# The product with w_out1 in groups of three tiles (384 columns), one block of output rows at a time

## Chip, core and metric

The kernel runs on one core of a Trainium2 chip. The metric is the device time of one launch in microseconds (us). It is written in Bass and Tile; the engines are TensorE (PE), VectorE (DVE), ScalarE (ACT), GpSimd (POOL) and SyncE (SP), which issues most DMAs. Each engine takes its instructions strictly in the order in which the program emits them.

## What is computed

The reference, cut to what matters:

```python
x = attention(q, k, v)                  # chunks of 64 rows, 8 x 8 heads, 4608 rows of 512 in all
h = x @ w_in                            # 512 -> 1024
e = np.exp(h - h.max(-1)); solu = h * e / e.sum(-1)
ln = (solu - mean) / np.sqrt(var + 1e-06) * g_ln
y = ln @ w_out                          # 1024 -> 512: "the product with w_out1"
h2 = y @ w_in2                          # 512 -> 2048
return (np.maximum(h2, 0) + alpha * np.minimum(h2, 0)) @ w_out2
```

## The kernel before

The 4608 rows are 36 tiles of 128. Phase 1 takes each tile through attention, the projection with `w_in`, SoLU, layer norm and the product with `w_out1`; the result `y` (transposed, 512 rows in four row blocks of 128) goes to DRAM. Phases 2 and 3 are the second feed-forward part and are not touched. Every fp32 product of this kind is three matmuls of rounded halves (`mm3`: high x high, high x low, low x high).

The order of all work in phase 1 is written by hand as tables of names with a tile number. `FIRST` lists the start (tiles 0 to 9), `STEP` is one step of the loop over tiles i = 10 to 35, in which `name+d` works on tile (or y step) i+d, and `LAST` is the end. The names that matter here: `q`, `qk`, `qm`, `qe`, `tr`, `te`, `pv`, `xn`, `xt` are attention; `xh` (ACT) and `xl` (DVE) split its result into high and low halves; `hm` is the projection (24 matmuls of 512 columns, line 483; below "projection t" for tile t); `hx` (DVE maximum), `he` (ACT exponential), `so` (DVE), `sq` (ACT square), `zv`, `pw` (POOL), `zs` (DVE) are SoLU and layer norm; `zt` transposes the result on PE into PSUM, `zh` (ACT) and `zl` (DVE) write its halves; `ya`, `yb` are the two halves of a y step, and `ye` (ACT) copies its result from PSUM and issues the store to DRAM. `conv` in `STEP` converts one unit of the second part's float64 weights (`p` on ACT, `l` on DVE, `s`, `a` on POOL) and, with `run_post`, splits earlier units (`hi` on ACT, `lo` on POOL). Steps 20, 24 and 28 (`twice`) convert a second unit, whose ACT work (`hi` of earlier units, then `p`) stands between `sq` and `xh`.

A projection can start only when `so` of the tile before has read its PSUM banks (`ps_h` has one buffer) and when its own `xh` is there; the loads and copies around it run ahead.

y groups: two tiles (`YT` = 2) share one pair of buffers `zh`, `zl` of 256 columns, three pairs in all. Each tile index s is a y step of two of the four row blocks of its group, `ya` the one and `yb` the other: 24 matmuls of 256 columns each. Both write one PSUM bank (`ps_y`, one buffer), and `ye` copies it in one ACT instruction of 512 columns. A second bank (`ps_y2`) is there for `LAST` alone. At the very start the float64 pieces of `w_in` and the halves of tiles 2 to 5 (`wraw`, `xe`) lie in the y buffers, which are not yet used.

Of the kernel before, what the change touches and what calls it, by code (L numbers as in the profile page):

```python
# [42 lines left out]
def order(text):  # L43
# [18 lines left out]
    f19 qs10 s16 zt3 h15 o15 l16 v11 hx4 s18 he4 p17 so4 A16 sq4 f21 s17 ya0 yb0 zv4 hm5 p20 ye0 zh3  # L62
    l17 ya1 yb1 pw4 l18 hm6 hx5 f22 he5 p19 qn10 a17 ye1 zs4 zl3 so5 a18 p21 xh8 sq5 S19 zv5 zt4 pw5
    h18 zs5 ya2 yb2 zh4 hx6 he6 h17 o18 zt5 zl4 l19 zh5 so6 o17 sq6 zv6 pw6 zl5 hm7 s20 zs6 zt6 ye2
    h16 hx7 he7 so7 xh9 xl8 zh6 sq7 ya3 yb3 zv7 S21 l20 pw7 zs7 hm8 tr10 zl6 hx8 zt7 qk11 a19 te10
    pv10 xl9 he8 f23 so8 sq8 zh7 hm9 qm11 zv8 ye3 zl7 xh10 hx9 ya4 yb4 pw8 qe11 zs8 he9 so9 sq9 h19
# [23 lines left out]
def tile_chunk_attention_solu_prelu(  # L90
# [75 lines left out]
    def phase1():  # L166
        with ExitStack() as c1, ExitStack() as c0:
# [416 lines left out]
            def yevac(s):
                assert ("yb", s) in done
                j, half = divmod(s, 2)
                y = yp.tile([128, 2, YG], F32, name="ysb", tag="ysb")
                nc.scalar.activation(out=y, in_=ypend.pop(s), func=AF.Copy)  # L588
# [520 lines left out]
```

## Time and profile before

| what | value |
|---|---|
| median of 3 runs (lowest to highest) | 1315.21 us (1315.11 to 1317.88) |
| the profiled execution: time, span | 1316.45 us, 1314.6 us |
| granted TensorE clock, mean over the span | 0.991 |
| busy PE, PEld, DVE, ACT, POOL | 96%, 89%, 72%, 52%, 25% of the span |
| phase 1 | 0 to 596.5 us |

The span runs from the first instruction to the last; the profiled execution's own time is 1.85 us longer. PE is busy nearly throughout, so what moves the end is PE work taken away or put in, and each wait that PE gains or loses. PEld are weight loads, which overlap the matmuls.

### The profile page before, as it was taken

The page shows a single profiled execution, that of the slowest core. Times are in us where ns is not written, and L with a number is a line of the kernel's source. Part 1 is how long each engine was busy: PE and PEld are TensorE (multiplying, and loading weights), DVE is VectorE, ACT ScalarE, POOL GpSimd, SP SyncE. Part 2 cuts the span into 40 slices and gives each one's busy share as a digit, 9 for nine tenths or more (in the row PEclk, how much of TensorE's full clock was granted, in tenths as well). Part 3 has the DMA queues.
Part 4 walks back from the last instruction along what each step waited for, and adds up shares of the span by engine and source line. Part 5 has one row for each costly group of instructions (what it writes and reads, how often), then busy time and mean ns, then how long its engine had stood idle before and what let it go on. Part 6 is the DMA issues. An engine that isn't in the chain of part 4 may idle for free. (4 is left out here: it accounts for less than half of the span.)

```text
span 1314.6 us, 21447 instructions
## 1 busy us (share of the span) xinstructions
PE 1264.9 (96%) x7968; PEld 1165.5 (89%) x7968; DVE 951.4 (72%) x1425; ACT 689.4 (52%) x1140; POOL 328.1 (25%) x311
## 2 busy tenths in 40 slices
PE   5889899999999999999999999999989999999998
PEld 4778789999889989899999999999989888888898
DVE  6996677776877666535777777777765968768684
ACT  4685355555555555434666666666534344434443
POOL 4574245343656464322020202110000000000000
PEclk9799999999999999999999999999998999999999
DMA  9774167675767573279442433427994738375462
GB/s 235 165 178 112 60 172 183 161 172 153 206 190 212 156 209 107 87 273 351 168 161 98 163 116 143 156 105 273 324 332 158 266 100 275 123 244 188 137 232 96
DMA packets 215496, 237.87 MB, mean 181 GB/s; under 512 B 89312, under 2 KB 174816, under 8 KB 213344
## 3 DMA queue, kind: packets, MB, share of 16 engines
q1 hardware_dynamic: 205440, 226.28, 55.5%
q10 hardware_dynamic: 9792, 9.44, 2.1%
q8 instruction: 63, 1.03, 0.3%
q0 software_dynamic: 160, 0.79, 0.1%
q14 instruction: 41, 0.34, 0.1%
HBM read 149.68 MB, written 86.77 MB: 180 GB/s over the span
## 5 line engine op out<-in xcount | busy, mean ns | idle before, releaser
L804 DVE SCALAR_TENSOR_TENSOR g<-ng,nal,g 128x384 f32<-128x384 f32 x192 | 126.2, 657 | 62.5 <-ACT g L682 62.4
L162 PE MATMUL yps<-zh,wo_h 128*128 128x256 f32 x576 | 167.4, 291 | 0.7 <-ACT ysb L588 0.7
L164 PE MATMUL yps<-zh,wo_l 128*128 128x256 f32 x576 | 162.9, 283 | 0.0
L163 PE MATMUL yps<-zl,wo_h 128*128 128x256 f32 x576 | 162.8, 283 | 0.0
L682 ACT ACTIVATE ng<-g 128x384 f32<-128x384 f32 x144 | 75.8, 526 | 131.7 <-DVE g L676 131.7
L765 PE MATMUL hz<-th,w 128*128 128x384 f32 x384 | 113.5, 336 | 4.4 <-DVE wv L676 4.2
L765 PE MATMUL hv<-th,w 128*128 128x384 f32 x384 | 113.5, 336 | 2.5 <-DVE g L676 2.3
L765 PE MATMUL hx<-th,w 128*128 128x384 f32 x384 | 112.9, 334 | 0.0
L162 PEld LDWEIGHTS yps<-zh,wo_h 128*128 128x128 f32 x576 | 110.3, 192 | 1.0 <-ACT ysb L588 0.9
L163 PEld LDWEIGHTS yps<-zl,wo_h 128*128 128x128 f32 x576 | 110.4, 192 | 0.1
L164 PEld LDWEIGHTS yps<-zh,wo_l 128*128 128x128 f32 x576 | 110.2, 191 | 0.0
L963 PE MATMUL oz<-rhi,w 128*128 128x512 f32 (+1 forms) x304 | 94.7, 372 | 0.6 <-DVE osb L676 0.6
L963 PE MATMUL ox<-rhi,w 128*128 128x512 f32 (+1 forms) x304 | 94.9, 373 | 0.0
L963 PE MATMUL ov<-rhi,w 128*128 128x512 f32 (+1 forms) x304 | 93.7, 369 | 0.0
L682 ACT ACTIVATE rhi<-rt 128x1024 fp32r<-128x1024 f32 (+1 forms) x56 | 54.6, 984 | 63.1 <-DVE rt L679 19.7
L679 POOL TENSOR_TENSOR yt<-y,y 128x384 f32<-128x384 f32 x24 | 26.9, 1143 | 238.8 <-DMA y<-yd 138.9
L682 ACT ACTIVATE g<-g 128x384 f32<-128x384 f32 x144 | 75.2, 522 | 3.1
L563 DVE TENSOR_TENSOR zl<-zt,zh 128x1024 fp32r<-128x1024 f32 x36 | 44.0, 1221 | 45.2 <-ACT zh L558 45.2
L765 PEld LDWEIGHTS hz<-th,w 128*128 128x128 f32 x384 | 70.7, 188 | 6.4 <-ACT th L682 4.7
L765 PEld LDWEIGHTS hv<-th,w 128*128 128x128 f32 x384 | 70.7, 188 | 4.6 <-DVE g L676 2.9
L483 PE MATMUL h<-wi_h,xh 128*128 128x512 f32 x256 | 70.9, 399 | 3.6 <-DVE sl L511 3.4
L679 DVE TENSOR_TENSOR rlo<-rt,rhi 128x1024 fp32r<-128x1024 f32 (+1 forms) x56 | 62.4, 1124 | 15.0 <-ACT rhi L682 14.7
(187 smaller groups left out, 3357.8 us busy)
## 6 DMA issues: line engine op xcount, KB each, us to landing
gd<-g SPq DMA_DIRECT2D x192, 192.0 KB, 1.9
w<-wid SPq DMA_DIRECT2D x8, 1792.0 KB, 9.4
w<-wod SPq DMA_DIRECT2D x8, 1792.0 KB, 9.9
rc<-gd SPq DMA_DIRECT2D x24, 512.0 KB, 3.9
rd<-gd SPq DMA_DIRECT2D x24, 512.0 KB, 4.8
raw<-in_moe_w_out SPq DMA_DIRECT2D x24, 511.8 KB, 4.3
qt<-in_q SPq DMA_DIRECT2D x36, 256.0 KB, 5.1
kbd<-in_k SPq DMA_DIRECT2D x72, 128.0 KB, 5.0
```

The costliest lines, as they stand in the source:

```text
L162: nc.tensor.matmul(o, lh, rh, start=first, stop=False)
L163: nc.tensor.matmul(o, lh, rl, start=False, stop=False)
L164: nc.tensor.matmul(o, ll, rh, start=False, stop=last)
L483: nc.tensor.matmul(ps[:, n], xh[:, kk], w[:, kk, 512 * n:512 * n + 512], start=(kk == 0 and w is wi_h), stop=False,)
L563: nc.vector.tensor_tensor(out=zl, in0=ps, in1=zh.bitcast(F32), op=ALU.subtract)
L679: eng.tensor_tensor(out=out, in0=a, in1=b, op=ALU.subtract)
L682: nc.scalar.activation(out=out, in_=in_, func=func, **k)
L765: nc.tensor.matmul(self.ps[x], w[:, a, i, k], d[:, k], start=(p not in CHAINED and k + j == 0), stop=(k == 1 and j == 2), skip_group_check ...
L804: nc.vector.scalar_tensor_tensor(out=self.g[t], in0=self.n[t], scalar=nal_sb[:, f:f + 1], in1=self.g[t], op0=ALU.mult, op1=ALU.add)
L963: nc.tensor.matmul(bank[key, m][:, :n], W[2 * j + k][:, a, i, 128 * m:128 * m + 128], d[:, k], start=(p not in CHAINED and j + k + q == 0) ...
```

## The change

A y group becomes three tiles (384 columns, `YT` = 3), with two pairs of buffers instead of three. The unit of work is one row block of a group: 24 matmuls of 384 columns. A group has three tile indices and four blocks: each index does one block, `ya` its first 12 matmuls and `yb` the other 12, and the first index of a group does one more block, `yc`, copied by `yd`. Each block is copied and stored by itself (384 columns). In the loop `yc` stands on PE between `qk` and `pv`, `yd` on ACT between `qe` and `so`. 1728 matmuls of 256 columns become 1152 of 384 columns; 36 copies and stores become 48. Of the tables `FIRST` and `LAST` a few entries are shown; how they move the instructions stands below.

```diff
-YT = 2
+YT = 3
 YG = 128 * YT
-YL = 6
...
-    f19 qs10 s16 zt3 h15 o15 l16 v11 hx4 s18 he4 p17 so4 A16 sq4 f21 s17 ya0 yb0 zv4 hm5 p20 ye0 zh3
+    f19 qs10 s16 zt3 h15 o15 l16 v11 hx4 s18 he4 p17 so4 A16 sq4 f21 s17 yc0 zv4 hm5 p20 yd0 zh3
...
-    zv9 qs11 qn11 A20 pw9 xl10 zs9 zt8 o16
+    zv9 qs11 qn11 A20 pw9 xl10 zs9 ye3 zt8 ya4 yb4 o16
...
 STEP = order(
     """
-    q+3 v+3 ye-6 zh-2 zl-2 conv+0 hm+0 tr+1 te+1 qk+2 hx+0 he+0 qm+2 qe+2 pv+1 zt-1 xn+1 so+0 sq+0
+    q+3 v+3 ye-6 zh-2 zl-2 conv+0 hm+0 tr+1 te+1 qk+2 yc-5 hx+0 he+0 qm+2 qe+2 yd-5 pv+1 zt-1 xn+1 so+0 sq+0
     ya-5 conv+1 xt+1 xh+1 xl+1 zv+0 pw+0 qs+2 zs+0 yb-5
     """
 )
...
-            ztp = R("zt", YL // 2)
+            ztp = R("zt", 2)
...
-            rawt = [
-                ztp.tile([128, 2, 512, 4], U16, name=f"wraw{kk}", tag="zh" if kk % 2 == 0 else "zl")
-                for kk in range(K1)
-            ]
-            xt = [ztp.tile([128, 2, 2, NP, 128], F32R, name=f"xe{k}", tag=t) for k, t in enumerate(("zh", "zl"))]
+            rawt = [ztp.tile([128, 3, 512, 4], U16, name=f"wraw{k}", tag=t) for k, t in enumerate(("zh", "zl"))]
+            rx = ztp.tile([128, 3, 2, NP, 128], F32R, name="rx", tag="zh")
+            xe = ztp.tile([128, 3, 2, NP, 128], F32R, name="xe", tag="zl")
...
-            def ymm(s, m):
+            def block(s, extra):
+                j, r = divmod(s, YT)
+                return j, 0 if extra else 1 + r
+
+            def ymm(s, extra, k0, k1):
+                j, m = block(s, extra)
...
-                if m == 0:
-                    ypend[s] = ypools[(s + 1) % len(ypools)].tile([128, 2, YG], F32, name="yps", tag="yps")
+                if k0 == 0:
+                    ypend[j, m] = ypools[m % len(ypools)].tile([128, 512], F32, name="yps", tag="yps")[:, :YG]
...
-                for kk in range(KF1):
-                    mm3(ps, wo_h[:, kk, c], wo_l[:, kk, c], zh[:, kk], zl[:, kk], kk == 0, kk == KF1 - 1)
+                c = slice(m * 128, (m + 1) * 128)
+                for kk in range(k0, k1):
+                    mm3(
+                        ypend[j, m], wo_h[:, kk, c], wo_l[:, kk, c], zh[:, kk], zl[:, kk], kk == 0, kk == KF1 - 1
+                    )
...
+                yc=lambda s: s % YT or ymm(s, True, 0, KF1), yd=lambda s: s % YT or yevac(s, True),
```

Two places show how the order moves (the changed kernel's line numbers are shifted by a few). On ACT, from the exponential of tile 7 (line 503, then 506) to the square of tile 9 and the weight splits behind it; `ysb` is a copy of y, `eh,st<-h` an exponential, `eh,st<-sl` a square. Before:

```order
L503 ACTIVATE eh,st<-h,st 128x1024
L469 ACTIVATE xh<-xd 128x512
L558 ACTIVATE zh<-zt 128x8x128
L519 ACTIVATE eh,st<-sl,st 128x1024
...
L519 ACTIVATE eh,st<-sl,st 128x1024
L238 ACTIVATE hi<-f_1432 128x512
L238 ACTIVATE hi<-f_1103 128x512
L238 ACTIVATE hi<-s_1361 128x512
L588 ACTIVATE ysb<-yps 128x512
```

Now:

```order
L506 ACTIVATE eh,st<-h,st 128x1024
L597 ACTIVATE ysb<-yps 128x384
L599 DMA yd_65<-ysb 128x384
L472 ACTIVATE xh<-xd 128x512
L561 ACTIVATE zh<-zt 128x8x128
L522 ACTIVATE eh,st<-sl,st 128x1024
...
L522 ACTIVATE eh,st<-sl,st 128x1024
L237 ACTIVATE hi<-f_1358 128x512
L237 ACTIVATE hi<-f_1101 128x512
L597 ACTIVATE ysb<-yps 128x384
L599 DMA yd_65<-ysb 128x384
L237 ACTIVATE hi<-s_1313 128x512
```

A copy of y (`ye2`) stands ahead of the work behind the exponential of tile 7, and another (`ye3`) behind two splits.

On PE, from the end of projection 9 to projection 10 (each pair of lines 162 and 164, now 161 and 163, stands for a run of y matmuls: before one of 48, now two of 24 around `zt`). Before:

```order
L489 MATMUL h<-wi_h,xl 128x512 x8
L162 MATMUL yps<-zh,wo_h 128x256
...
L164 MATMUL yps<-zh,wo_l 128x256
L545 MATMUL zt<-ident,sl 128x128 x8
L483 MATMUL h<-wi_h,xh 128x512 x4
```

Now:

```order
L492 MATMUL h<-wi_h,xl 128x512 x8
L161 MATMUL yps<-zh,wo_h 128x384
...
L163 MATMUL yps<-zh,wo_l 128x384
L548 MATMUL zt<-ident,sl 128x128 x8
L161 MATMUL yps<-zh,wo_h 128x384
...
L163 MATMUL yps<-zh,wo_l 128x384
L486 MATMUL h<-wi_h,xh 128x512 x4
```

Here two blocks stand where one step stood. Ahead of it, one block follows each of projections 4, 5 and 6 instead of one step each, and two blocks follow projection 7 instead of one step.

## Rows read from the trace of the kernel before

**Rows 1.** Busy time by engine in a stretch of the loop, then clock, DMA share, GB/s

```profile
200.00:300.00 100.00, 100.00 (x788) 91.13 (x787) 71.00 (x120) 54.18 (x85) 43.28 (x38) 1.00 0.70 167
```

**Rows 2.** Timeline of PE, step 17: start, length, line, tiles, count

```profile
280.53 1.09 PE L483 MATMUL h<-wi_h,xh 128*128 128x512 f32 x4
...
287.46 1.04 PE L439 MATMUL xr<-vbd,ets 128*64 128x128 f32 x16
...
289.28 0.36 PE L162 MATMUL yps<-zh,wo_h 128*128 128x256 f32 x1
289.48 0.28 PE L163 MATMUL yps<-zl,wo_h 128*128 128x256 f32 x1
...
292.24 0.60 PE L459 MATMUL x<-ident,e 128*128 128x128 f32 x4
...
295.55 1.09 PE L483 MATMUL h<-wi_h,xh 128*128 128x512 f32 x4
```

**Rows 3.** Timeline of PE in phase 2, matmuls of 384 columns

```profile
651.00 0.33 PE L765 MATMUL hv<-th,w 128*128 128x384 f32 x1
...
652.04 0.33 PE L765 MATMUL hx<-th,w 128*128 128x384 f32 x1
```

**Rows 4.** Timeline of PE at the start: projections 6 to 11

```profile
121.95 1.09 PE L483 MATMUL h<-wi_h,xh 128*128 128x512 f32 x4
...
138.73 1.19 PE L483 MATMUL h<-wi_h,xh 128*128 128x512 f32 x4 [3.44 <-DVE sl L511]
...
152.57 1.09 PE L483 MATMUL h<-wi_h,xh 128*128 128x512 f32 x4
...
162.55 1.19 PE L483 MATMUL h<-wi_h,xh 128*128 128x512 f32 x4
...
174.69 0.48 PE L483 MATMUL h<-wi_h,xh 128*128 128x512 f32 x1
...
190.43 0.86 PE L483 MATMUL h<-wi_h,xh 128*128 128x512 f32 x3
```

**Rows 5.** Timeline of DVE: `so` of tile 5, attention's scaling in step 17

```profile
119.77 1.28 DVE L511 SCALAR_TENSOR_TENSOR sl<-h,st,eh 128x1024 f32<-128x1024 f32 x1
...
289.01 0.68 DVE L450 TENSOR_TENSOR e<-xr,r 128x512 f32<-128x512 f32 x1
```

**Rows 6.** Timeline of PE in LAST: the second y step, the first matmul of phase 2

```profile
566.73 0.38 PE L162 MATMUL yps<-zh,wo_h 128*128 128x256 f32 x1 [0.69 <-ACT ysb L588]
...
596.49 0.34 PE L765 MATMUL hx<-th,w 128*128 128x384 f32 x1
```

**Rows 7.** Timeline of ACT behind projection 9

```profile
172.86 1.15 ACT L519 ACTIVATE eh<-sl,st 128x1024 f32<-128x1024 f32 x1 [2.00 <-DVE st L514]
...
174.01 1.13 ACT L238 ACTIVATE hi<-f 128x512 fp32r<-128x512 f32 x2
```

**Rows 8.** Timeline of ACT in step 17: the square, then the split of x

```profile
291.56 1.15 ACT L519 ACTIVATE eh<-sl,st 128x1024 f32<-128x1024 f32 x1 [1.80 <-DVE st L514]
...
292.88 0.60 ACT L469 ACTIVATE xh<-x 128x512 fp32r<-128x512 f32 x1
```

**Rows 9.** Timeline of ACT, steps 21 and 24

```profile
354.54 0.58 ACT L469 ACTIVATE xh<-x 128x512 fp32r<-128x512 f32 x1
...
397.52 1.15 ACT L519 ACTIVATE eh<-sl,st 128x1024 f32<-128x1024 f32 x1 [1.80 <-DVE st L514]
...
401.01 0.59 ACT L469 ACTIVATE xh<-x 128x512 fp32r<-128x512 f32 x1
```

**Rows 10.** Timeline of PE: projections 21, 29 and 30

```profile
340.75 1.20 PE L483 MATMUL h<-wi_h,xh 128*128 128x512 f32 x4
...
461.82 1.14 PE L483 MATMUL h<-wi_h,xh 128*128 128x512 f32 x4
...
478.71 0.50 PE L483 MATMUL h<-wi_h,xh 128*128 128x512 f32 x1
```

**Rows 11.** Busy time by engine and clock in a stretch, as Rows 1

```profile
139.00:144.00 5.00, 5.00 (x16) 3.92 (x16) 2.46 (x3) 1.69 (x3) 1.68 (x2) 0.66 0.32 115
```

More of the change, by code (lines that the diff above doesn't have):

```diff
@@ L61 @@
     pv9 h14 hm4 qm10 a13 h13 f18 f17 v12 o12 O13 p16 o14 sq3 l15 zv3 qe10 A15 pw3 zs3 f20 p18 v10
-    f19 qs10 s16 zt3 h15 o15 l16 v11 hx4 s18 he4 p17 so4 A16 sq4 f21 s17 ya0 yb0 zv4 hm5 p20 ye0 zh3
[L63 to L66, printed above, removed]
-    zv9 qs11 qn11 A20 pw9 xl10 zs9 zt8 o16
+    f19 qs10 s16 zt3 h15 o15 l16 v11 hx4 s18 he4 p17 so4 A16 sq4 f21 s17 yc0 zv4 hm5 p20 yd0 zh3
+    l17 ya0 yb0 pw4 l18 hm6 hx5 f22 he5 p19 qn10 a17 ye0 zs4 zl3 so5 a18 p21 xh8 sq5 S19 zv5 zt4 pw5
+    h18 zs5 ya1 yb1 zh4 hx6 he6 h17 o18 zt5 zl4 l19 zh5 so6 o17 sq6 zv6 pw6 zl5 hm7 s20 zs6 zt6 ye1
+    ya2 yb2 h16 hx7 he7 so7 ye2 xh9 xl8 zh6 sq7 yc3 zv7 S21 l20 pw7 zs7 hm8 tr10 zl6 hx8 zt7 qk11 a19 te10
+    pv10 xl9 he8 f23 so8 sq8 zh7 hm9 qm11 zv8 yd3 zl7 xh10 hx9 ya3 yb3 pw8 qe11 zs8 he9 so9 sq9 h19
+    zv9 qs11 qn11 A20 pw9 xl10 zs9 ye3 zt8 ya4 yb4 o16
     """
@@ L567, in phase1, with yevac @@
             ypools = [ps_y]
-            def ymm(s, m):
-                j, half = divmod(s, 2)
-                assert ("zl", 2 * j + 1) in done and all(("o", u) in done for u in range(UI, UO))
+            def block(s, extra):
[3 more added lines that the diff above has]
+                j, m = block(s, extra)
+                assert ("zl", YT * (j + 1) - 1) in done and all(("o", u) in done for u in range(UI, UO))
                 zh, zl = ztt[j]
-                if m == 0:
-                    ypend[s] = ypools[(s + 1) % len(ypools)].tile([128, 2, YG], F32, name="yps", tag="yps")
+                if k0 == 0:
+                    ypend[j, m] = ypools[m % len(ypools)].tile([128, 512], F32, name="yps", tag="yps")[:, :YG]
                 else:
                     assert ("ya", s) in done
-                ps = ypend[s][:, m]
-                c = slice((2 * half + m) * 128, (2 * half + m + 1) * 128)
-                for kk in range(KF1):
-                    mm3(ps, wo_h[:, kk, c], wo_l[:, kk, c], zh[:, kk], zl[:, kk], kk == 0, kk == KF1 - 1)
-                if half and m:
-                    del ztt[j]
[L584 to L588, printed above, removed]
+                c = slice(m * 128, (m + 1) * 128)
[3 more added lines that the diff above has]
+                    )
+                if m == K1 - 1 and k1 == KF1:
+                    del ztt[j]
+            def yevac(s, extra):
+                j, m = block(s, extra)
+                assert ("yc" if extra else "yb", s) in done
+                y = yp.tile([128, YG], F32, name="ysb", tag="ysb")
+                nc.scalar.activation(out=y, in_=ypend.pop((j, m)), func=AF.Copy)
                 g, o = divmod(j * YG, 2 * SG)
-                nc.scalar.dma_start(out=y_dram[g][:, 2 * half:2 * half + 2, o:o + YG], in_=y)
+                nc.scalar.dma_start(out=y_dram[g][:, m, o:o + YG], in_=y)
             for t in (kbd[0], vbd[0]):
```

19 lines of the change are left out of this document (12 added, 7 removed).

## The prediction

> **What bounds the kernel now.** First the busy time by stretches: in the loop of phase 1 PE is busy for all of 100 us at full clock while VectorE has 71, ScalarE 54 and GpSimd 43 of it [rows 1]. So PE's own work sets the time there, as long as the work of the other engines that PE needs back stays shorter than PE's work in between. The timeline of PE in one step shows how the 15.02 us from projection 17 to projection 18 (280.53 to 295.55) are spent, and where its two y pieces lie [rows 2]. The timelines of ScalarE and VectorE show how close they run behind it [rows 5, 8]. The start is another matter: before projection 7 PE stands still for 3.44 us, waiting for VectorE (`so`, line 511) [rows 4]. There PE work is free, and taking it away is worth nothing.
>
> **The price of a y matmul.** In rows 2 the y matmuls start 0.12 us apart: from 289.48 to the transposes at 292.24 there are 23 starts in 2.76 us. A piece of 24 takes 289.28 to 292.24, 2.96 us: 24 x 0.12, and 0.08 for its first one behind transposes. Phase 2 has 384 columns against other weights: six starts from 651.00 to 652.04, 0.1733 us each [rows 3]. So 256 columns cost 0.120 and 384 cost 0.1733: 0.0533 for each 128 and 0.0133 fixed. The product costs 1728 x 0.120 = 207.4 us before and 1152 x 0.1733 = 199.7 after: 7.7 us less PE work. [...]
>
> A block is now 24 x 0.1733 = 4.16 us, in the loop 4.24 in one piece or 2 x 2.16 in two. The 12 additional pieces (`yc`) add 0.08 each, 1 us in all at most; those in the loop are in the lengths below.
>
> **Steps of the loop.** Without y a step has 15.02 - 2 x 2.96 = 9.10 us of PE work. Two steps of three now take 9.10 + 2 x 2.16 = 13.42 (1.60 less), the third 13.42 + 4.24 = 17.66 (2.64 more). Steps 11 to 34 hold 16 short ones and 8 long ones: -25.6 + 21.1 = -4.5 us, if PE never waits. Does it wait? The next projection needs `xh`, on ScalarE behind `sq`. In step 17 `sq` starts 11.03 us after the projection (291.56) and `xh` ends at 293.48, 12.95 after it; PE came 2.07 us later [rows 8]. That chain hangs on the projection (maximum, exponential, `so`, `sq`), not on y, so a short step leaves 13.42 - 12.95 = 0.5 us: no wait. In a long step `pv` comes 4.24 us later (6.93 + 4.24 = 11.17 after the projection), lasts about 1.0, and VectorE's scaling of it (`xn`) stands ahead of `so`; before, `xn` started at 289.01 and `sq` 2.55 us behind [rows 5]. `sq` then starts at about 11.17 + 1.0 + 0.2 + 2.55 = 14.9, `xh` ends near 16.8, under 17.66: no wait. The additional copy `yd` stands on ScalarE between `qe` and `sq` and waits for `yc`; `sq` has to wait longer anyway, which hides it. Without that cover it would cost its half microsecond eight times over.
>
> The double steps 20, 24 and 28 are different. There two splits and a second unit's conversion stand between `sq` and `xh`: in step 24 `sq` starts at 397.52 and `xh` ends at 401.60, 4.08 us later [rows 9]. With `sq` at 11.03, `xh` ends at 15.11: PE's 15.02 just about covered that. A short step 24 reaches the next projection after 13.42 and waits 1.7. Step 28 is short too; I take it at 1.5, its splits being a little shorter. Step 20 is long: 14.9 + 4.08 = 18.98 against 17.66, a wait of 1.3. Before, the three had waits of 0.4 together. Step 21 follows one: `xh` ended at 355.12, 14.37 after projection 21 (340.75) [rows 9, 10], because VectorE was late from step 20; short, it waits 0.9. Step 29 took 16.89 before (461.82 to 478.71) [rows 10], 1.9 more than the rule, for the same lateness; it is a long step now and absorbs it. Net: 1.7 + 1.5 + 1.3 + 0.9 - 0.4 - 1.9 = +3.1 us. The loop: -4.5 + 3.1 = -1.4.
>
> **The start.** Before, three y steps stood ahead of projection 7; now three blocks, 4.16 instead of 5.76 us each. What PE saves there it waits, since `so` of tiles 4, 5 and 6 decide. Only projection 6 comes earlier: it started at 121.95 behind y, and `so` of tile 5 ended at 121.05 [rows 4, 5], so up to 0.8 us is won, and I carry it through to projection 7 at 137.9 (the chain in between starts at projection 6). The work left out there is put in later:
> - Projection 7 to 8 took 13.84 us with one step (5.84). Two blocks now, 2 x 4.16 + 0.08, and between them the copy `ye2`, since there is one PSUM bank. The same handover in `LAST` left PE idle for 0.69 us [rows 6]; I take 0.75. 13.84 - 5.84 + 8.40 + 0.75 = 17.2: projection 8 at 155.1.
> - Projection 8 to 9 held no y: 9.98, as before. Projection 9 at 165.1.
> - Projection 9 to 10: `ya3 yb3`, `zt8`, `ya4 yb4`. The second block waits for `ye3`, which stands on ScalarE behind `sq` of tile 9 and two splits. `sq` started 172.86 - 162.55 = 10.31 us behind projection 9, the splits end at 175.14, 12.59 behind it [rows 4, 7]; with 0.6 for the copy the block starts 13.2 after projection 9, about 2.5 us after PE is ready for it. With 4.2 for the block projection 10 comes after 17.4, at 182.5; before it came at 174.69.
> - Projection 10 to 11 took 15.74 because VectorE came late; with projection 10 so much later it won't be, and the step is short: 13.42. Projection 11 at 195.9 instead of 190.43: +5.5 us.
>
> The other edits of the start cost nothing: the pieces of `w_in` in other buffers have the same loads in the same order; `zh` of tile 3 must now wait for projection 5 (its buffer holds the halves of tile 5), but ScalarE waits for VectorE there anyway. DMAs: 12 more stores of y on ScalarE's queue, none on SP's.
>
> **The end.** From projection 35 on there were six y steps (34.6 us), now eight blocks (33.3): -1.3. Phase 2 began without a wait at 596.49 [rows 6], and its operands are prepared from rows of y stored long before, so this is kept. The one wait at the handover of the bank (0.69) stays.
>
> **Sum.** +5.5 - 1.4 - 1.3 = +2.8 us, and 0.3 for a little less luck with the clock (below): +3.1. The profiled execution took 1316.45, 1.24 over the median of the runs; I put the sum on both alike: 1319.6 for an execution like it, **1318.3 us** for the median.
>
> **Bounds of what no row shows.** How far y of 384 columns differs from phase 2's: from 0.1733 to 1.5 x 0.120 = 0.180, 0 to +7.7 us; I take the former, a row of the same engine and width. The handovers behind `ye2` and `ye3`: from 0.69 each [rows 6] to the 3.44 of the longest wait here [rows 4]; I take 0.75 and 2.5. Together these move the sum from 1.9 less to 3.6 more.
>
> **Rivals.**
> (A) *Faster: the postponed blocks cost nothing.* If the blocks behind projections 7 and 9 fell into waits that PE has there anyway, the start would keep its own saving (8 blocks for 6 steps: -1.3), and the kernel ends at -1.3 - 1.4 - 1.3 = -4.0, 1311.2 us. For it: PE did wait in the start. Against it: the wait of 3.44 lies ahead of the postponed blocks, and behind it projection 8 followed y without an idle time in its row. It decides if projection 11 starts before about 190. 0.10.
> (B) *No change: the double steps don't wait.* If ScalarE reaches `xh` of steps 20, 24, 28 in time, the loop comes to -4.5 - 1.9 - 0.4 + 0.9 = -5.9 instead of -1.4: 1313.8. For it: ScalarE is half idle. Against it: in step 24 it goes from `sq` to `xh` without an idle time in its rows. 0.22.
> (C) *Slower still: the clock.* PE idles for about 5.5 us around the transposes ahead of projection 7 and 2.5 ahead of `ya4`. Before, after the 3.44 us wait, the clock granted from 139 to 144 was 0.66 of full [rows 11], part of the time at 1.2 instead of 2.4 GHz: 5 x 0.34 = 1.7 us. Once or twice more makes 1320.0 to 1321.7. 0.18. The Trainium skill (TensorE: Matmul & The Clock Gate, "Part 1: The HAM clock gate") says that the throttled state is the default and activity releases it; the row agrees.
> (D) *The width is no saving.* With the matmul's time in proportion to its columns, 0.180, nothing is saved on PE: +7.7, 1326.0. Rows 3 speak against it. 0.03. [...]
>
> **Chances.** My forecast has 0.45, by itself from 1316.3 to 1320.3; others 0.02. A measurement of this kernel tells about 0.2% (2.6 us) from no change. The forecast lies near that bound (1317.8): of its 0.45 I give 0.27 to slower, 0.18 to the same. With C and D slower has 0.48; with B and the rest the same has 0.41; A makes 0.11 faster. Range 1313.5 to 1321.2: it holds the forecast, B and most of C.
>
> **What will show it.** Rows of y matmuls 0.173 apart. Projections 11 and on: intervals of 13.4, 13.4, 17.7. Projection 11 near 196, with an idle PE ahead of the second blocks behind projections 7 and 9, put down to the copy `ysb`. Steps 20, 24 and 28 at about 19.0, 15.2 and 15.0. Phase 2 starts near 599.5. I am wrong if projection 11 starts before 193, if the double steps keep the rule, or if phase 2, which isn't touched, takes another time.

## The result, and the profile after

The changed kernel takes 1335.27 us (median of four runs, 1330.28 to 1336.05) where the kernel before took 1315.8 in the same session: a ratio of 1.0139, 95% interval 1.0115 to 1.0163. It is slower by some 19 us; the forecast was 1318.3, at most 1321.2. The profiled execution has a span of 1334.2 us and took 1336.0.

The matmul count fell as the change says, and PE's busy time did not. The sums on the page of the kernel before (busy us, share of the span, count):

```profile
PE 1264.9 (96%) x7968; PEld 1165.5 (89%) x7968; DVE 951.4 (72%) x1425; ACT 689.4 (52%) x1140; POOL 328.1 (25%) x311
```

The page of the changed kernel, first its sums, then the three groups of y matmuls (busy, mean ns of one, idle time before them; matmuls overlap, so the mean is longer than the 174 ns from one start to the next):

```profile
PE 1266.0 (95%) x7392; PEld 1157.9 (87%) x7392; DVE 950.2 (71%) x1425; ACT 689.2 (52%) x1152; POOL 327.1 (25%) x311
...
L161 PE MATMUL yps<-zh,wo_h 128*128 128x384 f32 x384 | 134.5, 350 | 3.6 <-ACT ysb L597 3.6
L163 PE MATMUL yps<-zh,wo_l 128*128 128x384 f32 x384 | 128.8, 335 | 0.0
L162 PE MATMUL yps<-zl,wo_h 128*128 128x384 f32 x384 | 128.8, 335 | 0.0
```

The timeline of PE shows where the time went. These rows answer to [rows 4] and [rows 6] (L486 is the projection, L776 phase 2, L974 phase 3); they are the first matmuls of projections 4, 7, 8, 9, 10, 11 and 35, of phase 2 and of phase 3. The second fence has the three of the kernel before that no group ahead shows: projections 4 and 35 and phase 3.

```profile
99.54 0.48 PE L486 MATMUL h<-wi_h,xe 128*128 128x512 f32 x1
...
141.67 2.08 PE L486 MATMUL h<-wi_h,xh 128*128 128x512 f32 x4 [3.19 <-DVE sl L514]
...
160.18 1.08 PE L486 MATMUL h<-wi_h,xh 128*128 128x512 f32 x4
...
170.18 0.50 PE L486 MATMUL h<-wi_h,xh 128*128 128x512 f32 x1
...
187.51 0.39 PE L486 MATMUL h<-wi_h,xh 128*128 128x512 f32 x1
...
201.46 0.39 PE L486 MATMUL h<-wi_h,xh 128*128 128x512 f32 x1
...
566.90 1.08 PE L486 MATMUL h<-wi_h,xh 128*128 128x512 f32 x4
...
608.33 0.33 PE L776 MATMUL hx<-th,w 128*128 128x384 f32 x1
...
977.79 0.33 PE L974 MATMUL ox<-fhi,w 128*128 128x384 f32 x1
```

```profile
96.03 0.48 PE L483 MATMUL h<-wi_h,xe 128*128 128x512 f32 x1
...
553.78 0.40 PE L483 MATMUL h<-wi_h,xh 128*128 128x512 f32 x1
...
956.56 0.33 PE L963 MATMUL ox<-fhi,w 128*128 128x384 f32 x1
```

| stretch | before, us | after, us | difference | forecast |
|---|---|---|---|---|
| start to projection 4 | 96.03 | 99.54 | +3.5 | 0 |
| projections 4 to 11 | 94.40 | 101.92 | +7.5 | +5.5 |
| projections 11 to 35 (the loop) | 363.35 | 365.44 | +2.1 | -1.4 |
| projection 35 to phase 2 | 42.71 | 41.43 | -1.3 | -1.3 |
| phase 2 | 360.07 | 369.46 | +9.4 | 0 |
| phase 3 to the end of the span | 358.04 | 356.41 | -1.6 | 0 |

The largest term is phase 2, in which no line of code is changed. Two of its units have waits that the kernel before does not have (timeline of PE, then of DVE):

```profile
629.99 0.45 PE L776 MATMUL hx<-th,w 128*128 128x384 f32 x1 [2.77 <-ACT s L693]
...
641.07 0.45 PE L776 MATMUL hx<-th,w 128*128 128x384 f32 x1 [2.37 <-ACT s L693]
```

```profile
627.45 0.56 DVE L687 TENSOR_TENSOR g<-hz,u 128x384 f32<-128x384 f32 x1 [5.15 <-DMA gd<-g]
...
632.60 0.56 DVE L687 TENSOR_TENSOR g<-hv,wv 128x384 f32<-128x384 f32 x1 [1.08 <-DMA gd<-g]
...
637.80 0.56 DVE L687 TENSOR_TENSOR g<-hz,u 128x384 f32<-128x384 f32 x1 [2.38 <-DMA gd<-g]
```

PE waits for ScalarE, which waits for VectorE, and VectorE waits until stores of `g` (`gd<-g`) free one of the six buffers of `g`. Of the units of 42 matmuls the third and the fourth take 11.5 and 12.0 us where the kernel before has 7.3 and 7.7. Why are the stores late? The queue of SP, first of the kernel after, then of the kernel before: `w<-wid` are loads of the weights of phase 2, 1792 KB each. A row of several DMAs runs from the first issue to the end of the last.

```profile
608.40 1.27 SPq L712 DMA_DIRECT2D w<-wid  x3
...
615.11 1.32 SPq L820 DMA_DIRECT2D gd<-g  x2
616.48 5.80 SPq L738 DMA_DIRECT2D y<-yd  x4
622.38 4.86 SPq L820 DMA_DIRECT2D gd<-g  x2
```

```profile
585.09 11.91 SPq L701 DMA_DIRECT2D w<-wid  x3
603.28 1.31 SPq L809 DMA_DIRECT2D gd<-g  x2
604.64 2.00 SPq L727 DMA_DIRECT2D y<-yd  x4
```

Before, the first two of these three loads are issued 11.4 and 11.0 us ahead of phase 2 (596.49) and the third at its start; now all three are issued at its start (608.33), and the first stores of `g` follow 6.7 us later, when the first load has not landed yet. The view of DMA issues of these two stretches (KB each, median us to landing) shows what that costs the stores: 12.0 us after the change, 1.9 before.

```profile
gd<-g SPq DMA_DIRECT2D x2, 192.0 KB, 12.0
```

```profile
gd<-g SPq DMA_DIRECT2D x3, 192.0 KB, 1.9
```

In these stretches every DMA of SP's queue lands behind the one issued ahead of it: after the change the third load lands at 626.85 and the two stores at 627.36 and 627.87; before, the third load lands 0.55 us after the first store is issued. The Trainium skill (DMA: Bandwidth & Descriptors, "Queues, rings and completion order") says that a DMA engine consumes the descriptors of one issuing queue in the order of the ring, and that a later one may finish first all the same; here none did. The order of this queue is not the whole cause, though. A store of y of the same size on ScalarE's queue, issued at 609.05 amid the three loads, took 10.4 us as well, and the one ahead of it (604.89) 1.9:

```profile
yd<-ysb ACTq DMA_DIRECT2D x1, 192.0 KB, 10.4
```

No run separates what the order of the queue does to the stores from what the traffic of the loads does on either queue.

What moved the loads is in the built program (its tile addresses), not in the diff's lines. Phase 2 puts its weight tiles over the memory that phase 1 has done with, and a load waits for the last reader of what lay there. The tile of block 2 lies at bytes 214816 to 229152 of each partition. Before, there were three buffers of `zl` of 8192 bytes, and the topmost (208672 to 216864) held the last group but one. Now there are two of 12288, and the upper one (204576 to 216864) holds the last group, which the last y matmul before phase 2 reads. So theory R: **the reload waits for the last group**. Its rival S: in the built program the DMAs take eight completion semaphores in turn, each waiting for the one before it on the same semaphore, and twelve more stores turn that round by four places, so that stores may now wait for a slow load.

### The profile page after: what moved, and what is told of

It reads as the page before. It is cut to its first block, busy times and chain, and to the rows that moved or that the text cites. A ratio compares the mean times of both kernels' runs of the same rounds, so it can differ in the third digit from the quotient of the medians.

```text
span 1334.2 us, 20332 instructions
## 1 busy us (share of the span) xinstructions
PE 1266.0 (95%) x7392; PEld 1157.9 (87%) x7392; DVE 950.2 (71%) x1425; ACT 689.2 (52%) x1152; POOL 327.1 (25%) x311
## 5 line engine op out<-in xcount | busy, mean ns | idle before, releaser
L161 PE MATMUL yps<-zh,wo_h 128*128 128x384 f32 x384 | 134.5, 350 | 3.6 <-ACT ysb L597 3.6
L163 PE MATMUL yps<-zh,wo_l 128*128 128x384 f32 x384 | 128.8, 335 | 0.0
L162 PE MATMUL yps<-zl,wo_h 128*128 128x384 f32 x384 | 128.8, 335 | 0.0
L776 PE MATMUL hz<-th,w 128*128 128x384 f32 x384 | 114.3, 338 | 4.7 <-DVE wv L687 4.7
L776 PE MATMUL hx<-th,w 128*128 128x384 f32 x384 | 113.1, 335 | 5.1 <-ACT s L693 5.1
L776 PE MATMUL hv<-th,w 128*128 128x384 f32 x384 | 114.2, 338 | 3.5 <-DVE g L687 3.3
L974 PE MATMUL ox<-rhi,w 128*128 128x512 f32 (+1 forms) x304 | 94.9, 373 | 0.8 <-ACT rhi L693 0.8
L974 PE MATMUL oz<-rhi,w 128*128 128x512 f32 (+1 forms) x304 | 93.8, 369 | 0.8 <-DVE osb L687 0.8
L974 PE MATMUL ov<-rhi,w 128*128 128x512 f32 (+1 forms) x304 | 93.7, 369 | 0.0
L486 PE MATMUL h<-wi_h,xh 128*128 128x512 f32 x256 | 72.0, 403 | 10.0 <-ACT xh L472 4.5
L161 PEld LDWEIGHTS yps<-zh,wo_h 128*128 128x128 f32 x384 | 72.2, 188 | 6.2 <-ACT ysb L597 4.7
L776 PEld LDWEIGHTS hz<-th,w 128*128 128x128 f32 x384 | 71.2, 189 | 7.2 <-ACT th L693 4.7
L776 PEld LDWEIGHTS hv<-th,w 128*128 128x128 f32 x384 | 71.2, 189 | 6.3 <-DVE g L687 4.6
L776 PEld LDWEIGHTS hx<-th,w 128*128 128x128 f32 x384 | 70.7, 188 | 5.8 <-ACT s L693 5.8
L522 ACT ACTIVATE eh<-sl,st 128x1024 f32<-128x1024 f32 x36 | 41.4, 1151 | 61.3 <-DVE st L517 60.9
L162 PEld LDWEIGHTS yps<-zl,wo_h 128*128 128x128 f32 x384 | 72.3, 188 | 0.1
```

The source lines that it names most:

```text
L161: nc.tensor.matmul(o, lh, rh, start=first, stop=False)
L162: nc.tensor.matmul(o, lh, rl, start=False, stop=False)
L163: nc.tensor.matmul(o, ll, rh, start=False, stop=last)
L486: nc.tensor.matmul(ps[:, n], xh[:, kk], w[:, kk, 512 * n:512 * n + 512], start=(kk == 0 and w is wi_h), stop=False,)
L522: nc.scalar.activation(out=e, in_=s, func=AF.Square, bias=st[:, 4:5], accum_out=st[:, 5:6])
L776: nc.tensor.matmul(self.ps[x], w[:, a, i, k], d[:, k], start=(p not in CHAINED and k + j == 0), stop=(k == 1 and j == 2), skip_group_check ...
```

## The experiments

Each stretch of the profiled executions, in us, and the times of all runs (median; ratio to the kernel before in the same session, 95% interval). The names are those of the parts below.

| kernel | to proj. 4 | 4 to 11 | loop | to phase 2 | phase 2 | phase 3 | median | ratio |
|---|---|---|---|---|---|---|---|---|
| a_reload_early | 95.5 | 101.0 | 365.4 | 41.4 | 360.4 | 356.9 | 1326.28 | 1.0082 (1.0059 to 1.0105) |
| b_reload_late | 97.5 | 93.6 | 363.4 | 42.7 | 367.6 | 357.2 | 1323.73 | 1.0057 (1.0037 to 1.0077) |
| a_lanes | 97.7 | 101.9 | 365.4 | 41.4 | 367.9 | 356.4 | 1331.92 | 1.0122 (1.0100 to 1.0144) |
| a_first | 96.9 | 94.4 | 365.5 | 41.4 | 368.8 | 356.4 | 1325.58 | 1.0089 (1.0066 to 1.0111) |
| a_conv | 96.9 | 101.7 | 366.2 | 41.4 | 367.2 | 356.5 | 1334.38 | 1.0134 (1.0114 to 1.0154) |
| b_conv | 98.3 | 95.5 | 363.3 | 42.7 | 359.7 | 357.0 | 1315.81 | 0.9999 (0.9986 to 1.0012) |
| a_both | 98.0 | 94.5 | 365.5 | 41.4 | 360.4 | 358.8 | 1318.77 | 1.0020 (1.0005 to 1.0035) |
| a_all | 97.7 | 95.8 | 366.0 | 41.4 | 359.6 | 356.8 | 1319.76 | 1.0024 (1.0008 to 1.0040) |
| a_spread_only | 95.6 | 103.6 | 377.2 | 41.4 | 368.7 | 357.1 | 1344.20 | 1.0218 (1.0202 to 1.0235) |
| a_spread | 96.3 | 92.2 | 378.4 | 41.4 | 359.9 | 356.0 | 1326.17 | 1.0090 (1.0066 to 1.0113) |
| a_xn | 95.9 | 94.2 | 366.7 | 41.4 | 359.6 | 356.2 | 1317.72 | 1.0019 (1.0001 to 1.0036) |
| b_xn | 97.8 | 93.4 | 365.3 | 42.7 | 360.3 | 358.2 | 1317.17 | 1.0009 (0.9995 to 1.0023) |
| a_place_only | 98.3 | 102.6 | 361.6 | 42.8 | 368.3 | 356.3 | 1331.23 | 1.0123 (1.0103 to 1.0144) |
| a_place | 97.8 | 94.7 | 361.6 | 42.8 | 360.2 | 356.4 | 1314.32 | 0.9992 (0.9980 to 1.0005) |
| a_best | 96.0 | 92.2 | 361.6 | 41.4 | 359.6 | 359.1 | 1311.48 | 0.9972 (0.9961 to 0.9982) |
| b_twice | 96.6 | 93.2 | 365.3 | 42.7 | 359.9 | 356.6 | 1317.58 | 1.0018 (1.0007 to 1.0030) |

The first column settles one term at once: up to projection 4 the kernels with the buffers of before (b_ and before: 96.0 to 98.3) and those with the buffers of after (95.5 to 99.5) lie in one range. The 3.5 us there are scatter from execution to execution, and so are the 1.6 of phase 3 (355.97 to 359.11 in all). The loop, the end and, but for its reload, phase 2 repeat within some tenths.

### Phase 2: where the reload may start

**a_reload_early**: the changed kernel, the last group moved from under the first reload.

```diff
-ztp = R("zt", 2)
+ztp = R("zt", 1)
-rawt = [... name=f"wraw{k}", tag=t) for k, t in enumerate(("zh", "zl"))]
-rx = ... tag="zh")
-xe = ... tag="zl")
+rx = ... tag="zh1")
+xe = ... tag="zl1")
+rawt = [... name=f"wraw{k}", tag=t) for k, t in enumerate(("zh0", "zl0"))]
...
-                        ztp.tile([128, KF1, YG], F32R, name="zh", tag="zh"),
-                        ztp.tile([128, KF1, YG], F32R, name="zl", tag="zl"),
+                        ztp.tile([128, KF1, YG], F32R, name="zh", tag=f"zh{j % 2}"),
+                        ztp.tile([128, KF1, YG], F32R, name="zl", tag=f"zl{j % 2}"),
...
-            for b in (2, 7, 3, 6, 5, 4):
+            for b in (2, 3, 7, 6, 5, 4):
```

> The changed kernel with the z tiles placed so that the last group (tiles 33 to 35) lies below the first two weight tiles that phase 2 reloads (blocks 2 and 3), and with the second of these put next to the first. Nothing else moves; the DMAs keep their order. Theory R (the reload of blocks 2 and 3 waits for the last group of y, and the stores of g queue behind it): the two loads are issued near the end of block ya32 yb32, some 26 us before phase 2 instead of at its start; units 3 and 4 of phase 2 take 7.3 to 7.7 us instead of 11.5 and 12.0; phase 2 takes 360 to 362 us to the start of phase 3 instead of 369.5; the whole 1326 to 1328. Rival S (twelve more stores turn the round of the DMA semaphores, so that stores of g wait for a load of weights of the same semaphore): the semaphores stay as they are, so units 3 and 4 stay at 11 to 12 us and the whole at 1335.

Measured: 1326.28 us, phase 2 at 360.4. The queue of SP (its phase 2 starts at 603.37): the first loads are issued 16.6 us ahead of it, which is four blocks, the last group's, and not 26 as I had expected. It is enough: the third and fourth units take 7.28 and 7.76 us. The first two stores of `g` land after 2.1 us. DVE's wait for `gd<-g` is 0.5 us in all, where it was 8.6.

```profile
586.79 17.09 SPq L712 DMA_DIRECT2D w<-wid  x3
...
610.16 1.31 SPq L820 DMA_DIRECT2D gd<-g  x2
611.52 1.99 SPq L738 DMA_DIRECT2D y<-yd  x4
```

**b_reload_late**: the converse, the kernel before with the tile of block 2 over the last group.

```diff
-            for b in (2, 7, 3, 6, 5, 4):
+            for b in (7, 2, 3, 6, 5, 4):
```

> The kernel before, with one tuple changed: the weight tile of block 2 is put where that of block 7 was, so that it lies over the z tiles of the last group. Its load then has to wait for the last block of y. Theory R: blocks 2 and 3 load from the start of phase 2 on, units 3 and 4 slow down as in the changed kernel (by 7 to 9 us together), and the time rises to 1322 to 1325. Rival S: the semaphores are as before, so the time stays at 1315 to 1318. Its profile is also a second look at the first 100 us of the kernel before: projection 4 starts near 96 us if the 3.5 us there belong to the change, up to 100 if they are scatter.

Measured: 1323.73 us, and phase 2 takes 367.6. Its second, third and fourth units take 8.4, 9.5 and 12.0 us. Its queue of SP (phase 2 at 597.23) and DVE's wait (5.6 us in three times, 8.6 in the changed kernel) are of the same kind, though no y matmul and no store is changed:

```profile
597.31 1.27 SPq L701 DMA_DIRECT2D w<-wid  x3
604.03 1.31 SPq L809 DMA_DIRECT2D gd<-g  x2
605.39 5.95 SPq L727 DMA_DIRECT2D y<-yd  x4
```

```profile
DVE g L676 <- DMA gd<-g: 5.6, 3, 2.5
```

**a_lanes**: the changed kernel, the round of semaphores turned back.

```diff
+                dm=lambda i: nc.scalar.dma_start(out=dm_dram[:, i:i + 1], in_=g_sb[:, i:i + 1]),
...
-    ... ye31 ya32 yb32 sy0 sy1 ...
+    ... ye31 dm0 dm1 dm2 dm3 ya32 yb32 sy0 sy1 ...
```

> The changed kernel with four DMAs of 512 bytes on ScalarE's queue before phase 2, which nothing waits for: they turn the round of the DMA semaphores back to what it was before the change. Theory R: nothing changes in phase 2, 1334 to 1337. Rival S: units 3 and 4 go back to 7.3 to 7.7 us and the time to 1326 to 1328.

Measured: phase 2 stays at 367.9, its third and fourth units at 12.8 and 9.5 us. The whole is 1331.92, 3 us under the changed kernel and under what R expected; the profiled execution has 1.9 of that ahead of projection 4, where all kernels scatter, and 1.5 in phase 2. The kernels with a late reload and the round as in the change have 367.2 to 369.5 there, so the turn of the round has no part that these runs can show. Nor could it have much: in a round of eight the store that shares its semaphore with the third load is the eighth DMA behind it wherever the round stands. That store waits 2.4 us for the load after the change (it is issued at 626.91, the load lands at 626.85) and 2.1 in a_lanes; in the kernel before the load has landed by then (603.83, the store at 607.25). Theory R holds, in both directions.

### The first tiles: the order

**a_first**: two blocks and two evictions at other places in the hand-written order.

```diff
-... yb1 zh4 hx6 he6 h17 ... zl5 hm7 s20 zs6 zt6 ye1
-    ya2 yb2 h16 hx7 ...
+... yb1 zh4 hx6 he6 ye1 h17 ... ya2 yb2 zl5 hm7 s20 zs6 zt6
+    h16 hx7 ...
-... zs8 he9 so9 sq9 h19 ... zs9 ye3 zt8 ya4 yb4
+... zs8 he9 ye3 so9 sq9 h19 ... zs9 zt8 ya4 yb4
```

> The changed kernel with two places of the first tiles' order mended: block ya2 yb2 (with the eviction ye1 ahead of it) goes in front of projection 7, where TensorE stood idle 3.2 us, and eviction ye3 goes in front of the square of tile 9, since TensorE waited 2.2 us for a tile of yps. If the extra time between projections 7 and 11 comes of this order: projection 8 comes 3 to 4 us earlier, projection 11 5 to 6 us, the whole at 1329 to 1331. Rival (the chain of DVE and ScalarE sets these steps whatever the order is): projection 11 within 1.5 us of what it was, 1334 to 1336.

Measured: projections 4 to 11 take 94.4 us instead of 101.9, all of the 7.5 that the change had cost there. The whole is 1325.58, below the 1329 to 1331 expected: I had counted 5 to 6 us for the order, and 2.6 us of the profiled execution's gain lie ahead of projection 4, where all kernels scatter. PE's waits in that stretch, after the change (first fence) and in a_first (second):

```profile
PE h L486 <- DVE sl L514: 6.2, 3, 3.2
PE yps L161 <- ACT ysb L597: 2.8, 2, 2.2
```

```profile
PE h L486 <- DVE sl L514: 3.1, 2, 2.4
PE yps L161 <- ACT ysb L597: 2.1, 1, 2.1
```

The wait for `sl` ahead of projection 7 is filled with a block. The clock follows: granted 0.97 of full in the stretch from 100 to 200 us after the change, 1.00 in a_first (busy time by engine, then clock, DMA share, GB/s):

```profile
100.00:200.00 100.00, 87.74 (x480) 77.15 (x479) 61.94 (x98) 46.13 (x75) 32.58 (x30) 0.97 0.36 105
```

```profile
100.00:200.00 100.00, 91.84 (x530) 81.67 (x528) 67.67 (x104) 49.80 (x82) 38.67 (x35) 1.00 0.42 119
```

**a_both**: the two mends together.

> The changed kernel with both edits that gained: the z tiles placed for the early reload, and the mended order of the first tiles. If they are two separate losses, the gains add: phase 2 at 360.4, projections 4 to 11 at 94.4, the whole 9.0 and 8 to 9.7 us below 1335: 1316.5 to 1319. If one has hidden part of the other: over 1321.

Measured: 1318.77 us; both stretches keep what they had gained. The whole is now 0.2% above the kernel before.

### The loop: why so little

In the loop PE waits 4.5 us for `xh`, in or behind the double steps (waits of PE in the loop, after the change):

```profile
PE h L486 <- ACT xh L472: 4.5, 4, 1.5
```

**a_conv** moves the second conversion behind everything that the next projection needs, **b_conv** the same in the kernel before, **a_all** the same on top of a_both.

```diff
-    ya-5 conv+1 xt+1 xh+1 xl+1 zv+0 pw+0 qs+2 zs+0 yb-5
+    ya-5 xt+1 xh+1 xl+1 zv+0 pw+0 qs+2 zs+0 conv+1 yb-5
```

> The changed kernel with the second conversion of the double steps (20, 24, 28) moved behind everything that the next projection waits for (xh, xl, zs). In the changed kernel steps 20, 21, 24, 28 and 29 are 1.2, 0.9, 1.7, 1.4 and 0.6 us longer than steps of their kind. If that is the conversion standing ahead of xh on ScalarE while the step has only one block of y to cover it: steps 24 and 28 take 13.5 to 13.7 us, step 20 near 18.0, the loop from projection 11 to 35 is 4 to 5.5 us shorter than 365.45, and the whole 1329 to 1331. Rival (the conversion's work on ScalarE, VectorE and GpSimd delays the next step just as much wherever it stands): the loop stays within 1.5 us of 365.45, and the whole at 1333 to 1336.

> The kernel before with the same move of the second conversion. Its even steps of 15.02 us cover more of the wait: its loop of 363.35 us is only 2.9 over 24 such steps. If the uneven steps make the double steps dear in the changed kernel, this gains at most 1.5 to 2.9 us here: 1313 to 1315. If the move gains as much as in the changed kernel (5 us), unevenness is not what matters.

> As the run before, with the second conversion moved too. If all three add: 1311 to 1314.5, which is below the kernel before by 1.5 to 5 us: the saving of the wider matmuls (some 0.1 us for each step in the loop) and of the end (1.3 us), and what the kernel before loses in its own double steps. If the third gains nothing: 1316 to 1319, no better than before.

Measured: the loop of a_conv takes 366.2 us, no less than before the move, and a_all 366.0. Steps 20, 24 and 28 do fall to the length of their kind (17.98, 13.49, 13.49), and the steps behind them pay: 21 and 22 take 14.96 and 15.09, and 25 takes 16.27. PE's wait for `xh` falls to 0.8 us, and a wait for `ets`, which `te` copies on ScalarE for the next tile, takes its place:

```profile
PE xr L442 <- ACT ets L418: 4.6, 3, 2.6
```

The rival was right. In the kernel before the move does nothing (0.9999).

**a_spread_only** and **a_spread**: the blocks spread over the three steps (36, 36, 24 matmuls). A block is begun in one step and finished in the next, ahead of `xr`.

```diff
+yc=((0, 0, 8), (1, 4, 8), None), ya=((1, 0, 2), (2, 0, 4), (3, 0, 4)), yb=((1, 2, 4), (2, 4, 8), (3, 4, 8)),
+yd=(0, 1, None), ye=(None, 2, 3),
...
-            twice = {20, 24, 28}
+            twice = {20, 24, 27}
```

For each place (`yc` behind the scores, `ya` and `yb` as before) and each of the three steps this gives the block and the range of its eight slices of `KF1`. The first blocks of `LAST` change their order with it.

> The changed kernel with the four blocks of a group spread more evenly over the loop's three steps: 36, 36 and 24 matmuls where there were 48, 24 and 24 (the second block is begun in the first step and finished in the second), and with the double steps at 20, 24 and 27, which all have 36. If it is the short steps that make the double ones dear: the waits for xh (4.4 us in the loop) go, the loop from projection 11 to 35 takes 360 to 363 us instead of 365.45, and the whole 1330 to 1332.5. Rival (the double steps cost the same wherever they stand, or the cut block costs as much in changes between operations as it saves): the loop stays above 364.5.

> As the run before, with the z tiles placed for the early reload, the mended order of the first tiles, and one more eviction there (ye2) put ahead of the exponential of tile 7, since TensorE waited 2.1 us for it. If all add: 3 to 5 us off 1318.8 for the loop and 1 to 2 for the eviction, 1312 to 1315: below the kernel before. If the loop gains nothing: 1317 to 1319, and the change at its best costs nothing and brings nothing.

Measured: a clear miss, 12 us slower in the loop. Half of it is in PE's waits: 10.5 us for `xh`, ten of them, 6.0 more than after the change.

```profile
PE h L486 <- ACT xh L472: 10.5, 10, 3.1
```

Most of the rest is the price of the cut blocks: without the waits three steps take 16.06, 16.00 and 13.49, together 45.55 us, where the change has 44.96, some 4.7 us in eight groups. As to the waits, work put ahead of `xr` delays the chain that ends in `xh`; a_place, below, puts it behind. The timeline of DVE in a long step of the changed kernel shows the delay, the scaling of `xr` (L453) with the SoLU operations (L511 to L514) queued behind it:

```profile
303.90 0.69 DVE L453 TENSOR_TENSOR e<-xr,r 128x512 f32<-128x512 f32 x1 [3.97 <-PE xr L442]
304.51 0.14 DVE L511 TENSOR_SCALAR st<-st 128x1 f32<-128x1 f32 x1
...
304.89 1.28 DVE L514 SCALAR_TENSOR_TENSOR sl<-h,st,eh 128x1024 f32<-128x1024 f32 x1
```

**a_xn** (on top of a_both, with `ye2` ahead of `hx7`) exchanges the two on DVE and takes 20, 23, 26 as double steps; **b_xn** is the exchange in the kernel before.

```diff
-    ... pv+1 zt-1 xn+1 so+0 sq+0
+    ... pv+1 zt-1 so+0 xn+1 sq+0
```

> The changed kernel with the early reload and the mended order of the first tiles (with ye2 moved, which brought 2.3 us between projections 4 and 11 in the run before), the blocks again as in the change (48, 24, 24 matmuls), but with the SoLU operations of a tile ahead of the scaling of xr in VectorE's order, and the double steps at 20, 23 and 26, which all have two blocks. In the long steps VectorE waits 4.0 us for xr, which stands behind the postponed block on TensorE, and the chain SoLU, square, xh waits with it. If this is what makes the double steps dear: xh of a long step ends near 15.3 us instead of 16.8, double steps cost under 0.5 us, the loop takes 360.5 to 363 us instead of 365.45, and the whole 1311.5 to 1315. Rival (the late scaling then delays the transposes of x and xh as much): the loop stays at 364.5 to 366 and the whole at 1315 to 1318.

> The kernel before with the same exchange of SoLU and scaling. No block stands ahead of xr here, so VectorE does not wait there, and the steps are bound by TensorE. Theory: loop 362 to 363.5 us, the whole within 2 us of the kernel before. If it gains over 2 us, the exchange is an improvement of its own and no remedy of the change.

Measured: the loop stays at 366.7, since `xh` of a long step needs `xr` itself and still ends 16.7 us after the projection. PE no longer waits for `xh`, but 4.9 us for the scaled `xr` (`e`) ahead of the transposes of x. b_xn took 1317.17, no measurable change, though its loop is 1.9 us longer (step 29 takes 19.4), against what I expected. For a_xn the rival was right.

```profile
PE x L462 <- DVE e L453: 4.9, 2, 2.4
```

**a_place_only** and, with a_both and `ye2`, **a_place**: the postponed block behind `xr`.

```diff
-    ... qk+2 yc-5 hx+0 he+0 qm+2 qe+2 yd-5 pv+1 zt-1 xn+1 so+0 sq+0
+    ... qk+2 hx+0 he+0 qm+2 qe+2 pv+1 xn+1 yc-5 xt+1 zt-1 so+0 sq+0 yd-5
...
-                    else:
+                    elif (name, d) != ("xt", 1) or (i - 5) % YT == 0 or ("ya", i - 5) in done:
...
-            twice = {20, 24, 28}
+            twice = {20, 23, 26}
```

> The changed kernel with the postponed block of a long step behind xr on TensorE, and the transposes of x right behind it, ahead of those of zt; its eviction goes behind the square on ScalarE, and the double steps are the long steps 20, 23 and 26. If the block's place ahead of xr is what makes the double steps dear: xh of a long step ends near 14.8 us after its projection instead of 16.8, xh in a double step near 17.1 and so ahead of the next projection; PE waits for xh vanish; the loop takes 359.5 to 362 us instead of 365.45, and the whole 1329 to 1332. Rival (double steps cost 2 us each in a kernel with short steps wherever the block stands): the loop stays at 364.5 or more.

> The same with the early reload and the mended order of the first tiles. If the block's place is the cause: 1311 to 1314.5, below the kernel before by 2 to 5 us. If not: 1316 to 1319 as the other two versions with both mends, no better than before.

Measured: the loop takes 361.6 us instead of 365.4. `xh` now ends long before the next projection: in step 17 of a_place_only the projection is at 290.16, `xh` from 303.44 to 304.04, and the next projection at 307.82, 17.66 us on (timelines of PE and of ACT):

```profile
290.16 1.09 PE L486 MATMUL h<-wi_h,xh 128*128 128x512 f32 x4
...
297.10 1.04 PE L442 MATMUL xr<-vbd,ets 128*64 128x128 f32 x16
302.35 0.60 PE L462 MATMUL x<-ident,e 128*128 128x128 f32 x4
...
307.82 0.39 PE L486 MATMUL h<-wi_h,xh 128*128 128x512 f32 x1
```

```profile
303.44 0.60 ACT L472 ACTIVATE xh<-x 128x512 fp32r<-128x512 f32 x1 [0.40 <-ACT ysb L597]
```

Of the 3.8 us, 8 x 0.32 = 2.6 are the long steps, 17.66 for 17.98, and only some 1.2 the double ones: 20 and 21 now cost nothing, but 24 and 27, behind the double steps 23 and 26, take 15.4 instead of 13.5. With all three mends a_place is at 1314.32, no different from the kernel before.

**a_best** and **b_twice** put the double steps at 14, 17 and 20, a_best also the last `yd` ahead of the last square.

```diff
-            twice = {20, 23, 26}
+            twice = {14, 17, 20}
...
+                    if (name, i) == ("so", TILES - 1):
+                        emit("yd", i - 5)
```

> The version with all three mends, with the double steps at 14, 17 and 20 instead of 20, 23 and 26, and the eviction of the last postponed block ahead of the square of tile 35. If the early double steps cost nothing, as step 20 does: loop 357.5 to 359.5 us instead of 361.6, the end 1 us shorter, the whole 1308.5 to 1311.5, 0.3 to 0.5% below the kernel before. Rival (a double step costs 2 us wherever the load is on VectorE): loop 361 to 362, the whole at 1312.5 to 1314.5.

> The kernel before with its double steps at 14, 17 and 20. Its loop loses 2.9 us over 24 even steps; if the place of the double steps sets that, it gains 2 to 3 us, 1312.5 to 1314.5; if its even steps have cover enough and the loss stands elsewhere, 1315 to 1317.

Measured: the loop of a_best stays at 361.6 (steps 20 and 21 cost 4.4 us now), so the expectation on the loop fell, and that the whole is in the range that went with it is luck. The whole is 1311.48 us, 0.9972 of the kernel before (0.9961 to 0.9982): the fastest version. The end has 1.4 us of what it gains on a_place (41.4 for 42.8). Its start, 92.2 us from projection 4 to 11, is no gain of the edit: a_place has the same order there and took 94.7, of which 1.6 are projection 5 at a lower clock (granted 0.76 of full from 112 to 119). In the kernel before the same double steps cost 1.9 us more in the loop.

## Why the prediction was wrong, step by step

The profiled executions differ by +19.6 us where the terms of the forecast give +2.8. Of the 16.8 us in between 9.4 are phase 2, 3.5 the loop, 2.0 the stretch from projection 4 to 11, and 1.9 what the scatter ahead of projection 4 and in phase 3 leaves (+3.5 and -1.6).

**Phase 2 (forecast 0, measured +9.4): the step that failed first of all.** It reads "Phase 2 began without a wait at 596.49 [rows 6], and its operands are prepared from rows of y stored long before, so this is kept". I looked at the first matmul and at the rows of y, and not at the loads of the weights, which share their memory with the `z` tiles. The diff's smallest line, `R("zt", YL // 2)` to `R("zt", 2)`, three buffers to two, decided when these loads may start. a_reload_early takes the 9 us away and b_reload_late gives them to the kernel before. In front of it I had also written "The other edits of the start cost nothing", in which this line is counted; at the start it does cost nothing. That phase 2 takes another time was one of the signs of being wrong that the prediction names.

**The start (forecast +5.5, measured +7.5).** The mechanism was right, its sizes were a little small. Projections 4 to 7 came as expected (-0.6 for -0.8), 8 to 9 and 9 to 10 took 10.0 and 17.3 (10.0 and 17.4), with the wait for `ysb` that was foretold. Projections 7 to 8 took 18.5 (17.2), and 10 to 11 took 13.95 (13.42). In the former projection 7 itself lasted 1.2 us longer than in the kernel before: its first four matmuls take 2.08 us (row 141.67), those of projection 8 at full clock 1.08 (row 160.18). Behind the wait of 3.19 us the clock granted was 0.50 of full, the level of 1.2 GHz (before: 0.66 [rows 11]):

```profile
141.00:147.00 6.00, 5.33 (x13) 4.22 (x14) 3.23 (x6) 1.62 (x3) 1.67 (x2) 0.50 0.37 120
```

That is rival C, once. Where it falls is not fixed: in two other executions of this order (a_spread_only, a_place_only) projections 7 to 8 took 17.25, as forecast, and projections 9 to 10 18.9 and 18.8. The term is no price of the change as such either: with another order a_first is at the 94.4 us of the kernel before, and the four executions with `ye2` moved as well take 92.2 to 94.7.

**The loop (forecast -1.4, measured +2.1).** The double steps came as forecast: 20, 24 and 28 at 19.16, 15.15 and 14.93 (19.0, 15.2, 15.0), and in sum +2.9 us for the +3.1. The term that failed is the -4.5 of the steps without waits, which measured -0.8: three steps take 44.96 us (17.98 + 2 x 13.49) where they took 45.06 (3 x 15.02). The short step is 13.49 (13.42), the long one 17.98 (17.66), 16 x 0.07 + 8 x 0.32 = 3.7 us. The spacing of 0.1733 held; what I had too small is what a change from one kind of matmul to another costs. In step 17 after the change the postponed block takes 298.40 to 302.76, 4.36 us, where I had 4.24, and `sc` ahead of it and `xr` behind it take 0.10 and 0.06 longer than in step 18, which has no block there:

```profile
298.40 0.44 PE L161 MATMUL yps<-zh,wo_h 128*128 128x384 f32 x1
...
302.76 1.09 PE L442 MATMUL xr<-vbd,ets 128*64 128x128 f32 x16
```

The halves take 2.17 to 2.20 each, where I had 2.16. With the block behind `xr` a long step has just the 17.66.

**The end (forecast -1.3, measured -1.3)** was right.

**The rivals.** A (the postponed blocks cost nothing) fell: projection 11 starts at 201.46, not before 190; the mended orders show that one exists in which it about holds (92.2 to 94.7 us where the kernel before has 94.4). B (the double steps don't wait) fell, with four waits for `xh`. C held once, as above. D (no saving by the width) fell on its spacing, since y matmuls start 0.173 to 0.174 us apart as in phase 2; of the saving less is left than I had counted. None of the four names a wait outside phase 1.

**What stays open.** Double steps cost the kernel before some 2.9 us (363.35 for 24 steps of 15.02), and every version of the changed kernel 4 to 8 (its loop less eight times its two short steps and a long one). I have not found a place where the short steps hide them, and have not run even steps with all y work behind `xr`. The orders of the first tiles were mended for the changed kernel alone, so what its best version gains on the kernel before is no measure of the wider groups by themselves.

## What to carry to other kernels

When a change alters the number or the size of buffers, look at what is put on the same memory later, and at which of the old buffers is the last to be read: the price can fall into a stage that the diff does not touch. Large loads that start late delay the small stores issued behind or amid them, here on another queue too, and so the buffers that these stores free. Work that is to cover a chain of other engines has to stand behind the instruction that starts the chain; ahead of it the same work delays the chain by nearly its own length: `xh` of a long step ended 16.8 us after the projection with the block of 4.4 us ahead of `xr` and 13.9 with it behind, and that of a short step 12.8.

## What was unexpected of the hardware

Three loads of 1792 KB at once on SP's queue hold the stores of 192 KB behind them for 12.0 us, where they land after 1.9 with one load ahead that has all but landed; a store of the same size on ScalarE's queue is held for 10.4. A run of 24 matmuls of 384 columns takes 4.36 us between `sc` and `xr` (4.27 behind `xr` in a_place_only) and not 24 spacings, 4.16; two runs of 12 take 2 x 2.18. Versions of the changed kernel reach projection 4 between 95.5 and 99.5 us, execution by execution, while the five of them with the same loop repeat it within 0.1 us.
